# Conversion DMAs on GpSimd's queue, conversion steps in other iterations, a first pair started inside the first MLP, and another order inside a pair

## The chip, the cores and the metric

The kernel runs on one core of one Trainium2 chip. The metric is the device time of one execution in microseconds (us). TensorE (PE, its weight loads are PEld), VectorE (DVE), ScalarE (ACT), GpSimd (POOL) and SyncE (SP) each run their own list of instructions in order and wait for one another by semaphores; SP does nothing here but start DMAs (its queue is SPq).

## The reference

```python
kv = einsum('bhsd,bhse->bhde', k, v)            # q, k, v: 4 x 8 x 576 x 64, fp32
out = einsum('bhsd,bhde->bhse', q, kv)
attn = out / sqrt(mean(out * out, -1) + 1e-6) * g_norm
x = attn.transpose(0, 2, 1, 3).reshape(2304, 512)
gate = 1 / (1 + exp(-(x @ w_gate)))             # 512 -> 1536
y = (gate * (x @ w_val)) @ w_out                # 1536 -> 512, the first MLP
h = y @ w_in                                    # 512 -> 2048
g = max(h, 0) + log1p(exp(-abs(h)))
result = g @ w_out2                             # 2048 -> 512, the second MLP
```

All of it is fp32 in and out.

## The kernel before

**Products.** Each large product is made of three matmul passes over a high and a low part of both operands (`PASSES`, L22; `mm3`, L62). A tensor is split by an ACT copy to the high part (`split_hi`, L66) and a DVE subtraction for the low part (`split_lo`, L69).

**First MLP.** The 2304 tokens are cut into five tiles of 512, 512, 384, 384 and 512 (`TILES1`), each with 12 iterations, n = 0 to 59 in all. In iteration n PE multiplies x by a slice of the gate weights (12 matmuls into ps_g, `sigmoid` on ACT), by a slice of the value weights (12 into ps_v, `gated` L509 and `gated_lo` on DVE, a cast on ACT), and runs the output product of the iteration before (12 into yacc, `ffn1_out`). Other work is hung into this loop by `at_place(n, place, ...)`: "A", "B", "C" lie on PE behind the g, v and output products, "bg" and "b" behind the sigmoid and the gating, "end" ahead of the output product, "late" at the iteration's end. The attention of the next tile runs there, piece by piece: loads of q (16 DMAs a piece, L430) and of k and v (L252, L255), DVE transposes of q (L437), products po and kv_ps (L272), a root and a reciprocal (L481), the scaled rows of x.

**Conversion.** The weights of the second MLP arrive as 64-bit words and are made into fp32 on the chip, for j = 0 to 7, each an "i" part (w_in) and a "u" part (w_out2): `m_load` (4 or 2 DMAs, L582, L578), `m_a` (two ACT steps), `m_b` (two DVE steps of 128x1024, L596 and L599), for "i" also `m_sums` (four DVE adds that make the sums which the second MLP multiplies by), `m_h` (a cast on ACT), `m_l` (DVE), and `m_store` (L634, L628) into wi_dram and wu_dram. j takes iterations 12+5j to 16+5j, so the eight take 12 to 51. All these DMAs, and all others, are started by SP, in one line: a DMA that waits for its buffer or data holds those behind it. The raw words lie in home c0, m_f in c1 or c2, m_y in c2.

**Second MLP.** Three blocks of 768 tokens, 8 pairs each, 24 pairs. A pair forms 2 slices of h by seven products of 6 matmuls (128x384, two PSUM banks ps_b and ps_c), named by weight piece and sum of y: 11, 12, 22, S1 to S4 (`product`, L664). Copies on ACT (L1134, L1145, L1155, L1169) and additions on DVE (L1140, L1156, L1161) put them together. Softplus runs on ACT and DVE in steps of 128x768 (`s_abs` ... `s_lo`), and `out_group` (3 matmuls of 128x512, called a fill, 12 a pair) multiplies the pair before by w_out2 into oacc. The weights are read back by `feed_next` into `RING`, eight homes. The seven sums of y for a block lie in homes b0 to b6 (`COMBS`) as y_c; those of the next block are written over them when the last pair of a block is done with each (`combs`). `out_evac` copies oacc out and stores it.

**What sets the order.** The program text is the order of each engine. Names of lines that the prediction uses are in brackets above.

Of the kernel before, what the change touches and what calls it, by code (L numbers as in the profile page):

```python
# [30 lines left out]
def attention_moe_moe_kernel(ctx: ExitStack, tc: tile.TileContext, q, k, v, g_norm,  # L31
# [540 lines left out]
    m_x, m_f, m_y = {}, {}, {}  # L572

    def m_load(kind, j):
        m_x[kind, j] = x = block("c0", [P, 4, 256, 2], U32, "m_raw")
        if kind == "u":
            for f in range(2):
                nc.sync.dma_start(out=x[:, 2 * f:2 * f + 2].rearrange("p s c two -> p (s c two)"),  # L578
                                  in_=row_unit(w_out2, 2 * j + f))
        else:  # L580
            for f, kh, slot in ((1, 0, 0), (0, 0, 1), (0, 1, 2), (1, 1, 3)):
                nc.sync.dma_start(out=x[:, slot].rearrange("p (k m) two -> p k (m two)", k=2),  # L582
# [635 lines left out]
```

## Time and profile before

| | us |
|---|---|
| median of 3 runs (lowest, highest) | 949.48 (948.06, 953.69) |
| the profiled execution, its own time | 948.98 |
| its span in the profile | 947.2 |
| PE busy | 901.9 (95%) |
| DVE busy | 603.7 (64%) |
| ACT busy | 488.7 (52%) |
| POOL busy | 1.6 |

Three stretches of the span: tiles of 384 tokens, iterations 24 to 47, from 245 to 437.5 us; the last tile of the first MLP, from 437.5 to 534.8 us; the second MLP, from 534.8 us on. In the rows below, a line of the chain or of the timeline begins with the start and the length in us; "x12" is a count of instructions; a bracket holds the idle time of the engine before it and who ended it.

### The profile page before, as it was taken

The numbers are of one execution on the slowest core, as the hardware profiler recorded it, in microseconds if no ns is written. First come the engines' busy times: TensorE is split into PE (matmuls) and PEld (weight loads), VectorE is DVE, ScalarE is ACT, GpSimd is POOL, SyncE is SP. The second block draws the span as 40 slices with busy tenths as digits, with TensorE's granted clock in tenths as the row PEclk, the third lists the DMA queues.
The fourth block names the chain that finished last, engine by engine and source line by source line (L and its number), as shares of the span: only waits on it lengthen the run. The fifth ranks groups of instructions, "written<-read, shape, count | busy, mean of one in ns | idle before, by whom it ended". The sixth has DMA issues, their size and how long they took to land.

```text
span 947.2 us, 12188 instructions
## 1 busy us (share of the span) xinstructions
PE 901.9 (95%) x4701; PEld 785.0 (83%) x4701; DVE 603.7 (64%) x873; ACT 488.7 (52%) x771; POOL 1.6 (0%) x8
## 2 busy tenths in 40 slices
PE   8899999999988999999999989999799999799997
PEld 6687888788887989897888879888688988689896
DVE  4797846566875675687532256576675767657575
ACT  5887744445455454654322255556555555555553
POOL 0000000000000000000000000000000000000000
PEclk9999999999999999999999999999999999999999
DMA  9997367754678568755825536563286445265311
GB/s 303 271 338 234 133 216 230 215 199 172 194 225 268 206 173 264 225 203 205 283 72 196 185 125 240 182 247 153 90 295 236 190 166 219 79 258 207 148 45 67
DMA packets 108058, 188.50 MB, mean 199 GB/s; under 512 B 35936, under 2 KB 84320, under 8 KB 95712
## 3 DMA queue, kind: packets, MB, share of 16 engines
q1 hardware_dynamic: 106624, 186.94, 56.9%
q10 hardware_dynamic: 1376, 0.79, 0.3%
q8 instruction: 37, 0.61, 0.3%
q14 instruction: 21, 0.17, 0.1%
HBM read 148.90 MB, written 38.80 MB: 198 GB/s over the span
## 4 chain that ended last, share of the span: by engine, by line
PE 72%; DVE 10%; ACT 6%; DMA 6%; SPq 4%; issue 2%; DVEq 0%; ACTq 0%
PE oacc L62 18%; PE yacc L62 11%; PE ps_g L62 11%; PE ps_v L62 11%; PE ps_b L664 9%; PE ps_c L664 8%; DMA kv_raw<-in_v_dram 2%; SPq L117 1%; DMA m_raw<-in_moe_w_in_dram 1%; DVE y_c L69 1%; SPq L430 1%; DMA q_raw<-in_q_dram 1%; DVE ms L481 1%; DVE m_f L69 1%; DVE m_raw L596 1%
## 5 line engine op out<-in xcount | busy, mean ns | idle before, releaser
L62 PE MATMUL oacc<-w_up,g 128*128 128x512 f32 x864 | 221.0, 397 | 1.3 <-ACT g L66 0.7
L62 PEld LDWEIGHTS oacc<-w_up,g 128*128 128x128 f32 x864 | 162.6, 190 | 29.0 <-DVE g L69 1.2
L62 PE MATMUL ps_v<-x,w 128*128 128x512 f32 (+1 forms) x720 | 160.0, 370 | 3.1 <-DVE sg L509 1.8
L62 PE MATMUL yacc<-ghl,w 128*128 128x512 f32 (+1 forms) x720 | 162.6, 375 | 0.0
L62 PE MATMUL ps_g<-x,w 128*128 128x512 f32 (+1 forms) x720 | 160.3, 370 | 2.0 <-ACT x L396 0.9
L62 PEld LDWEIGHTS ps_g<-x,w 128*128 128x128 f32 x720 | 131.2, 189 | 20.4 <-DVE x L397 1.4
L62 PEld LDWEIGHTS ps_v<-x,w 128*128 128x128 f32 x720 | 129.5, 188 | 20.8 <-DVE sg L509 2.4
L62 PEld LDWEIGHTS yacc<-ghl,w 128*128 128x128 f32 x720 | 132.1, 191 | 16.9 <-DVE w L69 0.4
L664 PE MATMUL ps_b<-y_c,w_in 128*128 128x384 f32 x576 | 119.5, 341 | 13.9 <-ACT y_c L66 7.1
L664 PEld LDWEIGHTS ps_b<-y_c,w_in 128*128 128x128 f32 x576 | 103.1, 188 | 23.4 <-ACT y_c L66 8.8
L664 PE MATMUL ps_c<-y_c,w_in 128*128 128x384 f32 x432 | 89.8, 342 | 3.8 <-DVE c L1156 2.5
L503 ACT ACTIVATE sg<-ps_g 128x512 f32<-128x512 f32 (+1 forms) x60 | 33.3, 556 | 109.6 <-PE ps_g L62 105.1
L509 DVE TENSOR_TENSOR sg<-sg,ps_v 128x512 f32<-128x512 f32 (+1 forms) x60 | 37.9, 631 | 81.4 <-PE ps_v L62 77.7
L664 PEld LDWEIGHTS ps_c<-y_c,w_in 128*128 128x128 f32 x432 | 76.4, 190 | 12.8 <-DVE c L1156 7.9
L66 ACT CAST ghl<-sg 128x512 fp32r<-128x512 f32 (+1 forms) x60 | 34.6, 576 | 80.9 <-DVE sg L509 80.9
L671 ACT ACTIVATE e<-c 128x768 f32<-128x768 f32 x48 | 40.7, 847 | 64.0 <-DVE c L1161 63.3
L66 ACT CAST g<-c 128x768 fp32r<-128x768 f32 x48 | 40.2, 837 | 55.6 <-DVE c L696 55.6
L69 DVE TENSOR_TENSOR g<-c,g 128x768 fp32r<-128x768 f32 x48 | 45.8, 955 | 21.7 <-ACT g L66 21.7
L691 DVE SCALAR_TENSOR_TENSOR u<-u,ln 128x768 f32<-128x768 f32 x48 | 45.8, 954 | 15.5 <-ACT ln L683 15.4
L69 DVE TENSOR_TENSOR ghl<-sg,ghl 128x512 fp32r<-128x512 f32 (+1 forms) x60 | 38.2, 636 | 21.2 <-ACT ghl L66 20.9
L679 DVE TENSOR_SCALAR u<-e 128x768 f32<-128x768 f32 x48 | 26.7, 556 | 34.2 <-ACT e L675 34.2
L696 DVE TENSOR_TENSOR c<-c,u 128x768 f32<-128x768 f32 x48 | 46.0, 958 | 1.7
(124 smaller groups left out, 902.4 us busy)
## 6 DMA issues: line engine op xcount, KB each, us to landing
w_in<-wi_dram SPq DMA_DIRECT2D x42, 1024.0 KB, 6.8
w<-wo_dram SPq DMA_DIRECT2D x24, 1024.0 KB, 5.7
w_up<-wu_dram SPq DMA_DIRECT2D x24, 1024.0 KB, 4.8
m_raw<-in_moe_w_in_dram SPq DMA_DIRECT2D x32, 256.0 KB, 4.7
m_raw<-in_moe_w_out_dram SPq DMA_DIRECT2D x16, 512.0 KB, 4.2
wu_dram<-m_f SPq DMA_DIRECT2D x16, 512.0 KB, 3.2
w_raw<-in_moe_w_gate_dram SPq DMA_DIRECT2D x12, 512.0 KB, 8.8
w_raw<-in_moe_w_val_dram SPq DMA_DIRECT2D x12, 512.0 KB, 9.1
```

The source lines that it names most:

```text
L62: nc.tensor.matmul(out=ps, lhsT=lhs(a), rhs=rhs(b), start=start and n == 0, stop=stop and n == 2)
L66: nc.scalar.copy(out=hi, in_=src)
L69: nc.vector.tensor_tensor(out=lo, in0=src, in1=hi.bitcast(F32), op=ALU.subtract)
L117: nc.sync.dma_start(out=t, in_=unit(w, f))
L430: nc.sync.dma_start(out=t[32 * c:32 * c + 32, hp, :m].rearrange("p (g j) -> p g j", j=32), in_=q[b, 2 * hp + hh, s0:s0 + m, 32 * e:32 * e ...
L503: nc.scalar.activation(out=sg, in_=chain.pop(("g", t, i)), func=ACTF.Sigmoid)
L509: nc.vector.tensor_tensor(out=sg, in0=sg, in1=chain.pop(("v", t, i)), op=ALU.mult)
L664: nc.tensor.matmul(out=ps, lhsT=w[:, a, kk * P:(kk + 1) * P], rhs=y[:, b, kk], start=first and kk == 0 and n == 0, stop=kk == 1 and n == 2 ...
L671: nc.scalar.activation(out=e, in_=h_t[p][:, f], func=ACTF.Abs)
L679: nc.vector.tensor_scalar(out=u, in0=e_t[p, f], scalar1=1.0, scalar2=None, op0=ALU.add)
L691: nc.vector.scalar_tensor_tensor(out=u, in0=u, scalar=1.0, in1=ln_t.pop((p, f)), op0=ALU.subtract, op1=ALU.subtract)
L696: nc.vector.tensor_tensor(out=h, in0=h, in1=u_t.pop((p, f)), op=ALU.subtract)
```

## The change

**DMAs.** `m_load` and `m_store` are started by GpSimd (`nc.gpsimd`) and no longer by SP: 104 DMAs. For j from 5 on, the raw words and m_f of "u" have homes of their own (d0, d1), in room that the attention leaves.

**Iterations.** The rule 12+5j is replaced by the table `WHEN_J`. A row is (m_a and m_b of "i", m_sums, m_h and m_l of "i", m_a and m_b of "u", m_h and m_l of "u"); the last three rows have "u" one iteration behind "i".

**First pair.** Four products of pair 0 (11, 12, S2, S1) are in iteration 57, three (S3, S4, 22) in iteration 58, its softplus in 59.

**Sums of y.** Nine homes in turn instead of seven fixed ones, keyed by block, so that sums of the next block can be made in the last three pairs of a block (`gaps`). The ring has six homes instead of eight.

**Order in a pair.** 11, 12, S2, S1, S3, three fills, S4, 22, nine fills. A finished block is copied out in the second pair of the next. The last pair does its softplus in quarters of 128x384 (`quads`, `last_pair`), and the last groups are copied out one by one in the order 3, 4, 5, 0, 1, 2.

```diff
-    COMBS = ("11", "21", "T1", "T2", "22", "T3", "T4")
+    Y_HOME = ("b0", "b1", "b2", "b3", "b4", "b5", "b8", "b10", "b11")
...
     def m_load(kind, j):
-                nc.sync.dma_start(out=x[:, 2 * f:2 * f + 2].rearrange("p s c two -> p (s c two)"),
+                nc.gpsimd.dma_start(out=x[:, 2 * f:2 * f + 2].rearrange("p s c two -> p (s c two)"),
...
     def m_store(kind, j, a):
-                nc.sync.dma_start(out=wi_dram[g // 4][:, g % 4:g % 4 + m, a], in_=part[:, s:s + m])
+                nc.gpsimd.dma_start(out=wi_dram[g // 4][:, g % 4:g % 4 + m, a], in_=part[:, s:s + m])
...
-    RING = ("b7", "b8", "o0", "b9", "b10", "o1", "b11", "o2")
+    RING = ("b6", "b7", "o0", "b9", "o1", "o2")
...
-    for j in range(F2 // 2):
-        at_place(10 + 5 * j, "late", call(m_load, "i", j))
-        n = 12 + 5 * j
+    WHEN_J = ((9, 10, 11, 12, 13), (17, 18, 19, 20, 21), (25, 26, 28, 29, 30), (31, 32, 33, 34, 35),
+              (36, 37, 38, 39, 40), (48, 49, 50), (51, 52, 53), (54, 55, 56))
+    for j, (n, ns, nh, *nu) in enumerate(WHEN_J):
...
+    at_place(n0 + 9, "C", call(p_start, 0), call(p_11, 0), call(p_copy, 0), call(p_12, 0), call(p_add, 0, 0, 0, 0),
+             call(p_s2, 0), call(p_copy, 1), call(p_s1, 0))
+    at_place(n0 + 10, "A", call(p_s3, 0), call(p_copy, 2), call(p_add, 0, 1, 1, 2))
+    at_place(n0 + 10, "B", call(p_s4, 0), call(p_add, 0, 0, 1, 1))
+    at_place(n0 + 10, "C", call(p_22, 0), call(p_last, 0))
...
+            if j == NJ - 3:
+                return (call(y_sub, "T1", "12", "11", t_1), call(y_sub, "T2", "22", "T1", t_2)), \
+                       (call(y_diff, "T3", "22", "12", "12"),)
+            if j == NJ - 2:
+                return (call(y_split, "11"), call(y_split, "21")), (call(y_diff, "T4", "21", "T2", "21"),)
+            if j == NJ - 1:
+                return (call(y_split, "T2"), call(y_split, "T1"), call(y_hi, "T3"), call(y_hi, "22")), \
+                       (call(y_lo, "T3"), call(y_lo, "22"))
+        if j == 0 and p:
+            return (call(y_split, "T4"),), ()
...
+        p_start(p)
+        p_11(p)
+        s_lo(q, 0)
+        p_copy(0)
+        s_ln(q, 1)
+        for f in evac[:3]:
+            f()
+        p_12(p)
+        p_add(p, 0, 0, 0)
+        s_u2(q, 1)
+        p_s2(p)
+        s_sub(q, 1)
+        p_copy(1)
+        p_s1(p)
+        p_s3(p)
+        p_copy(2)
+        s_hi(q, 1)
+        p_add(p, 1, 1, 2)
+        s_lo(q, 1)
...
+        fill(3)
+        p_s4(p)
+        p_add(p, 0, 1, 1)
+        for f in gap_b:
+            f()
+        s_abs(p, 0)
+        s_exp(p, 0)
+        p_22(p)
+        p_last(p)
...
+        fill(99)
```

Place 1, SP around the loads of k, v and q for the last tile, with buffer numbers. First before, then after: L204 loads output weights of the first MLP, L255 k and v, L430 q, and L634 stores converted weights.

```order
L255 DMA kv_raw_2594<-in_k_dram 128x2x256
L255 DMA kv_raw_2594<-in_v_dram 128x2x256
L204 DMA w_2650<-wo_dram_90 128x2048
L634 DMA wi_dram_91<-m_y_2676 128x3x256
L634 DMA wi_dram_91<-m_y_2676 512x1x256
L255 DMA kv_raw_2711<-in_k_dram 128x2x256
L255 DMA kv_raw_2711<-in_v_dram 128x2x256
L634 DMA wi_dram_91<-m_f_2533 128x3x256
L634 DMA wi_dram_91<-m_f_2533 512x1x256
L255 DMA kv_raw_2745<-in_k_dram 128x2x256
L255 DMA kv_raw_2745<-in_v_dram 128x2x256
L430 DMA q_raw_2782<-in_q_dram 32x2x32 x16
```

```order
L255 DMA kv_raw_2563<-in_k_dram 128x2x256
L255 DMA kv_raw_2563<-in_v_dram 128x2x256
L204 DMA w_2624<-wo_dram_90 128x2048
L255 DMA kv_raw_2683<-in_k_dram 128x2x256
L255 DMA kv_raw_2683<-in_v_dram 128x2x256
L255 DMA kv_raw_2717<-in_k_dram 128x2x256
L255 DMA kv_raw_2717<-in_v_dram 128x2x256
L430 DMA q_raw_2759<-in_q_dram 32x2x32 x16
```

The four stores that stood between the loads of k and v are gone from SP; the loads keep their order.

They stand on POOL, whose list after the change reads here as follows (L593 and L589 load raw words, L645 and L639 store; j = 2 and the loads of j = 3 and of the "u" part).

```order
L593 DMA m_raw_2180<-in_moe2_w_in_dram 128x2x256 x4
L589 DMA m_raw_2362<-in_moe2_w_out_dram 128x1024 x2
L645 DMA wi_dram_91<-m_y_2566 128x2x256
L645 DMA wi_dram_91<-m_y_2566 512x1x256
L645 DMA wi_dram_91<-m_y_2566 128x256
L645 DMA wi_dram_91<-m_f_2344 128x2x256
L645 DMA wi_dram_91<-m_f_2344 512x1x256
L645 DMA wi_dram_91<-m_f_2344 128x256
L593 DMA m_raw_2722<-in_moe2_w_in_dram 128x2x256 x4
L639 DMA wu_dram_92<-m_f_2688 256x1x512 x2
```

POOL has no other work between them.

Place 2, PE at the end of the first MLP, first before, then after. The products ps_b and ps_c are those of pair 0 (before, from its tenth row on also of pair 1); the list of after begins at its first product.

```order
L62 MATMUL ps_v<-x,w 128x512 x12
L62 MATMUL yacc<-ghl,w 128x512 x12
L664 MATMUL ps_b<-y_c,w_in 128x384 x6
L664 MATMUL ps_c<-y_c,w_in 128x384 x6
L664 MATMUL ps_b<-y_c,w_in 128x384 x6
L62 MATMUL yacc<-ghl,w 128x512 x12
L664 MATMUL ps_c<-y_c,w_in 128x384 x6
L664 MATMUL ps_b<-y_c,w_in 128x384 x6
L664 MATMUL ps_c<-y_c,w_in 128x384 x6
L664 MATMUL ps_b<-y_c,w_in 128x384 x12
L664 MATMUL ps_c<-y_c,w_in 128x384 x6
L664 MATMUL ps_b<-y_c,w_in 128x384 x6
```

```order
L677 MATMUL ps_b<-y_c,w_in 128x384 x6
L677 MATMUL ps_c<-y_c,w_in 128x384 x6
L677 MATMUL ps_b<-y_c,w_in 128x384 x6
L677 MATMUL ps_c<-y_c,w_in 128x384 x6
L62 MATMUL ps_g<-x,w 128x512 x12
L677 MATMUL ps_b<-y_c,w_in 128x384 x6
L62 MATMUL ps_v<-x,w 128x512 x12
L677 MATMUL ps_c<-y_c,w_in 128x384 x6
L62 MATMUL yacc<-ghl,w 128x512 x12
L677 MATMUL ps_b<-y_c,w_in 128x384 x6
L62 MATMUL ps_g<-x,w 128x512 x12
L62 MATMUL ps_v<-x,w 128x512 x12
```

The seven products of pair 0 moved from behind the last ps_v to the place between the products of the last three iterations; after the last row shown come yacc x24 and the first product of pair 1.

Place 3, PE in pair 1, with buffer numbers, first before, then after. oacc is a fill, of pair 0; each product names the y_c that it reads.

```order
L664 MATMUL ps_b_4783<-y_c_4223,w_in_4536 128x384 x6
L664 MATMUL ps_c_4793<-y_c_4277,w_in_4584 128x384 x6
L664 MATMUL ps_b_4783<-y_c_4375,w_in_4584 128x384 x6
L62 MATMUL oacc_4816<-w_up_4538,g2_4784 128x512 x3
L664 MATMUL ps_c_4793<-y_c_4325,w_in_4584 128x384 x6
L62 MATMUL oacc_4817<-w_up_4538,g2_4784 128x512 x3
L664 MATMUL ps_b_4783<-y_c_4472,w_in_4630 128x384 x6
L62 MATMUL oacc_4818<-w_up_4538,g2_4784 128x512 x3
L62 MATMUL oacc_4819<-w_up_4538,g2_4784 128x512 x3
L664 MATMUL ps_c_4793<-y_c_4423,w_in_4630 128x384 x6
L62 MATMUL oacc_4820<-w_up_4538,g2_4784 128x512 x3
L664 MATMUL ps_b_4783<-y_c_4521,w_in_4584 128x384 x6
```

```order
L677 MATMUL ps_b_4788<-y_c_4167,w_in_4536 128x384 x6
L677 MATMUL ps_c_4799<-y_c_4225,w_in_4622 128x384 x6
L677 MATMUL ps_b_4788<-y_c_4402,w_in_4622 128x384 x6
L677 MATMUL ps_c_4799<-y_c_4346,w_in_4622 128x384 x6
L677 MATMUL ps_b_4788<-y_c_4521,w_in_4690 128x384 x6
L62 MATMUL oacc_4833<-w_up_4760,g2_4743 128x512 x3
L62 MATMUL oacc_4834<-w_up_4760,g2_4743 128x512 x3
L62 MATMUL oacc_4835<-w_up_4760,g2_4743 128x512 x3
L677 MATMUL ps_c_4799<-y_c_4461,w_in_4690 128x384 x6
L677 MATMUL ps_b_4788<-y_c_4577,w_in_4622 128x384 x6
L62 MATMUL oacc_4836<-w_up_4760,g2_4743 128x512 x3
L62 MATMUL oacc_4837<-w_up_4760,g2_4743 128x512 x3
```

The single fills between S2, S1 and S3 are gone, three fills stand together behind S3, and the rest behind 22.

## Rows read from the trace of the kernel before

**Rows 1.** Windows: stretch, its length, busy us (instructions) by engine, granted clock, DMA.

```profile
core 0: us, PE busy (x) PEld busy (x) DVE busy (x) ACT busy (x) POOL busy (x), PEclk, DMA share, GB/s
245.00:437.50 192.50, 177.15 (x1046) 168.46 (x1044) 133.05 (x235) 102.16 (x192) 0.00 (x0) 0.98 0.67 216
437.50:534.80 97.30, 97.30 (x432) 80.89 (x433) 39.24 (x52) 27.69 (x41) 0.00 (x0) 1.00 0.52 187
553.10:933.30 380.20, 367.91 (x1782) 324.53 (x1782) 251.03 (x327) 201.36 (x295) 0.00 (x0) 0.99 0.45 172
698.64:714.34 15.70, 15.70 (x80) 14.05 (x79) 10.01 (x13) 8.24 (x13) 0.00 (x0) 1.00 0.78 310
```

**Rows 2.** Chain of work: start us, us, engine, tile, line and count of matmuls.

```profile
332.38 2.08 PE ps_g L62 x12
...
535.99 1.04 PE ps_c L664 x6
...
642.34 4.80 PE oacc L62 x21
```

**Rows 3.** Waits of PE, 245 to 437.5 us: total, times, longest us.

```profile
PE po L62 <- ACT hl L66: 8.6, 10, 2.0
PE kv_ps L272 <- DMA kv_raw<-in_v_dram: 3.8, 2, 2.1
```

**Rows 4.** Chain of what released the stall at 274 us.

```profile
264.47 1.24 DVE m_f L599
...
265.76 0.37 SPq L582
...
267.71 2.07 SPq L430
```

**Rows 5.** Timeline, 274 to 432 us: start, us; in brackets idle time before, releaser.

```profile
274.29 0.81 PE L62 MATMUL po<-hl,kvb 128*128 128x160 f32 x3 [1.53 <-ACT hl L66]
...
295.33 0.98 SPq L634 DMA_DIRECT2D wi_dram<-m_y  x2
...
306.61 0.95 PE L272 MATMUL kv_ps<-kv_raw 128*64 128x64 f32 x20 [1.77 <-DMA kv_raw<-in_v_dram]
...
307.49 3.86 PE L62 MATMUL yacc<-ghl,w 128*128 128x384 f32 x12
...
424.72 1.22 DVE L596 SCALAR_TENSOR_TENSOR m_raw<-m_raw 128x1024 uint32<-128x1024 uint32 x1
...
432.08 2.35 PE L62 MATMUL ps_v<-x,w 128*128 128x384 f32 x12 [1.85 <-DVE sg L509]
```

**Rows 6.** Chain of work between the two MLPs.

```profile
534.92 1.06 PE ps_b L664 x6
...
543.49 0.57 DVE c L1156
...
553.09 1.82 PE ps_b L664 x6
```

**Rows 7.** Chain of work: fills of 21 matmuls around the two block boundaries.

```profile
698.64 4.80 PE oacc L62 x21
...
777.27 4.80 PE oacc L62 x21
...
834.34 4.80 PE oacc L62 x21
```

**Rows 8.** Waits of PE's weight loads, 553.1 to 933.3 us: total, times, longest.

```profile
PEld ps_c L664 <- DVE c L1156: 6.4, 21, 1.1
```

**Rows 9.** Timeline of PE in the last 20 us.

```profile
928.38 4.96 PE L62 MATMUL oacc<-w_up,g 128*128 128x512 f32 x21
...
935.36 8.00 PE L62 MATMUL oacc<-w_up,g 128*128 128x512 f32 x34 [0.61 <-DVE g L69]
```

**Rows 10.** Source line L634, its DMA issues on SP: ns minimum/median/maximum, first and last start.

```profile
L634 SPq DMA_DIRECT2D wi_dram<-m_f x20: 320/560/1575, 166.1 to 455.2; - x20
```

**Rows 11.** The page's costliest groups: busy us, mean ns, idle before.

```profile
L69 DVE TENSOR_TENSOR g<-c,g 128x768 fp32r<-128x768 f32 x48 | 45.8, 955 | 21.7 <-ACT g L66 21.7
```

More of the change, by code (lines that the diff above doesn't have):

```diff
@@ new lines, in attention_moe_moe_kernel, with p_open @@
+    at_place(n0 + 5, "end", call(y_split, "T1"), call(y_diff, "T2", "22", "T1", "T1"))
+    at_place(n0 + 6, "end", call(y_split, "T2"), call(y_diff, "T4", "21", "T2", "21"))
+    at_place(n0 + 7, "end", call(y_split, "22"))
+    at_place(n0 + 8, "end", call(y_split, "T3"))
+    at_place(n0 + 9, "b", call(y_split, "T4"))
+    for n in (7, 8, 9, 10, 11):
+        at_place(n0 + n, "late", feed_next)
+    p_c, p_t = {}, {}
+    def p_open():
+        more.close()
+        p2.append(ctx.enter_context(tc.tile_pool(name="p2a", bufs=1, side="right")))
+        p_t["t2"] = p2[0].tile([P, 2, HT], F32, tag="t2", name="t_2")
+        for n in range(3):
+            p_c[n] = block(f"c{n}", [P, 4 * 512], F32, "c")
@@ new lines, in h_of, with p_part, p_bank, p_copy @@
+    def h_of(p):
+        return p_c[p % 2][:, :2 * TM2].rearrange("p (f s) -> p f s", f=2)
+    def p_part(n):
+        return p_c[2][:, HT * n:HT * (n + 1)]
+    def p_bank(p, name):
+        pool, tag = (mm, "mm") if p else (atp, "at")
+        p_t[name] = pool.tile([P, 512], F32, tag=tag, name="ps_" + name)[:, :HT]
+    def p_copy(n):
+        nc.scalar.copy(out=p_part(n), in_=p_t["b"])
+    def p_add(p, f, th, n):
+        nc.vector.tensor_tensor(out=h_t[p][:, f, HT * th:HT * (th + 1)], in0=p_t["c"], in1=p_part(n), op=ALU.add)
@@ new lines, in p_last, with p_start, p_11, p_12 @@
+    def p_last(p):
+        nc.scalar.copy(out=h_t[p][:, 1, :HT], in_=p_t["b"])
+    def p_start(p):
+        h_t[p] = h_of(p)
+        p_bank(p, "b")
+    def p_11(p):
+        product(p, p_t["b"], "11", "11", True)
+    def p_12(p):
+        p_bank(p, "c")
+        product(p, p_t["c"], "12", "21", True)
+    def p_s2(p):
+        product(p, p_t["b"], "S2", "T2", False)
+    def p_s1(p):
+        product(p, p_t["c"], "S1", "T1", True)
+    def p_s3(p):
+        product(p, p_t["b"], "S3", "T3", False)
@@ L1066, in attention_moe_moe_kernel @@
             at.close()
+            more_pool.append(more.enter_context(tc.tile_pool(name="more", bufs=1, side="right")))
     assert not work
-    xs.close()
-    p2 = ctx.enter_context(tc.tile_pool(name="p2", bufs=1))
-    nc.scalar.preload_act_table_set("natural_log_exp_and_others")
-    ca, cb, cc = (block(f"c{n}", [P, 4 * 512], F32, "c") for n in range(3))
-    h_buf = [x[:, :2 * TM2].rearrange("p (f s) -> p f s", f=2) for x in (ca, cb)]
-    p1, u2, u3 = (cc[:, HT * n:HT * (n + 1)] for n in range(3))
@@ new lines, in attention_moe_moe_kernel @@
+    ffn1_out(*its[-1][1:])
+    feed_to(0)
+    for _ in range(2):
+        og = g1pool.tile([P, 2, 512], F32, tag="g", name="ob")
+        obs += [og[:, 0], og[:, 1]]
+    for p in range(1, NPAIR + 1):
+        q = p - 1
+        t, j = divmod(p, NJ)
+        evac = [call(out_evac, q - 1, s) for s in range(NS2)] if j == 1 and t else []
+        q_fill = [call(out_group, q, f, s) for f in range(2) for s in range(NS2)]
+        if p == NPAIR:
+            for n in range(NS2):
+                out_group(q, 0, n)
+            for n in (3, 4, 5, 0, 1, 2):
+                out_group(q, 1, n)
+                out_evac(q, n)
@@ L1181, in attention_moe_moe_kernel @@
         fill(99)
[L1182 to L1187 removed]
+        feed_to(p)
 _INS = ['q', 'k', 'v', 'g_norm', 'moe_w_gate', 'moe_w_val', 'moe_w_out', 'moe2_w_in', 'moe2_w_out']
```

264 lines of the change are left out of this document (151 added, 113 removed).

## The prediction

> **What bounds the kernel now.** I read the page first: PE is busy for 901.9 of 947.2 us, DVE for 603.7, ACT for 488.7. PE has the most work, and no PE work is added or removed, so whatever the change gains must come out of PE's gaps and of the stretches where PE runs at a lower clock. I then cut the span into stages with the windows view. The last tile of the first MLP has no gap (97.30 of 97.30 us at a granted clock of 1.00). The two tiles of 384 tokens have 15.35 us of gaps in 192.50, at a clock of 0.98. The second MLP from pair 1 on is busy for 367.91 of 380.20 us [rows 1]. The chain of work gives the dense pace there: 12 matmuls of 384 columns take 2.08 us, a product of 6 takes 1.04, and 21 matmuls of 512 take 4.80, so one of 512 takes 0.229 [rows 2]. A pair is 7 products and 36 fill matmuls: 7 × 1.04 + 36 × 0.229 = 15.5 us. A measured pair takes 15.70, with DVE busy for 10.01 and ACT for 8.24 of it [rows 1].
>
> The losses lie in five places. I cost each one against the profiled execution's own time, 948.98 us (1.78 outside its span of 947.2, and 0.5 below the median of 949.48; I call this the same).
>
> **A, the order within a pair: 4 us.** S4 waits for the addition L1156 that frees ps_c: 6.4 us over 21 pairs, 0.3 each [rows 8]. In the new order three fills stand between S3 and S4, 3 × 3 × 0.229 = 2.06 us, in which ACT's copy and that addition (0.57, [rows 6]) fit. A pair then runs at its floor of 15.5 instead of 15.7, and about 20 of the 23 pairs behind pair 0 are plain ones: 20 × 0.2 = 4. Between 0 and 6.4.
>
> **B, the two block boundaries: 17 us.** From the fill at 642.34 to that at 698.64 are 56.30 us for what would be three pairs of 15.70, 47.1, and a second entry makes one more step: 9.2 us lost [rows 2, 7]. At the other boundary, 777.27 to 834.34, it is 57.07 − 47.1 = 9.97 [rows 7]. Sum 19.2. In that time the splits of y's sums stand in the last pair and the first, since each has to wait for its home. With nine homes they are spread over three pairs, four of them in the fullest one. A split costs DVE 0.955 us (the nearest row, [rows 11], the same 768 columns), so DVE needs 10.01 + 4 × 0.955 = 13.8 of 15.5 us there, which fits. I leave 1 us at each boundary: 17. If all four splits stay unhidden at each, 19.2 − 2 × 3.8 = 11.6, so 12 to 19.
>
> **C, the way into the second MLP: 7 us.** Pair 0's first product is at 534.92, pair 1's at 553.09: 18.17 us [rows 6]. PE's work in between is 7 × 1.04 and the last 12 yacc matmuls at 0.229, 10.0 together, so 8.2 are lost while pair 1 waits for pair 0's softplus. In the new program the seven products stand between full products of the last iterations and the softplus lies beside iteration 59, in which DVE was busy for 39.24 of 97.30 us [rows 1]. Pair 1's first five products, 5.2 us, need nothing of it. I take 7, for one late step. If four DVE steps of 0.955 are still not covered it is 4.4, so 4 to 8.2.
>
> **D, the end: 1.6 us.** 21 matmuls begin at 928.38 and the last 34 at 935.36 [rows 9]. At 4.80 us for the 21 and 0.46 for two between them, 6.98 − 5.26 = 1.7 us are lost waiting for the last pair's softplus. Quarters of 384 columns should be ready by then: 1.6, between 0 and 1.7. The last copy and its store stay.
>
> **E, the stalls in the tiles of 384 tokens: 12 us.** The stretch holds 15.35 us of gaps and, at a mean clock of 0.98, 0.02 × 192.5 = 3.9 us of slow running: 19.2 [rows 1]. Most gaps are in po, 8.6 us, and in kv_ps, 3.8 [rows 3]. Two places show SP's one line as the cause. At 264.47 DVE runs its last step on c0's words; only then can SP start m_raw (265.76), and q's 16 loads behind it begin at 267.71; po then waits 1.53 us at 274.29 [rows 4, 5]. At 295.33 a store of m_y, which waits for the cast, stands ahead of the loads of k and v; kv_ps waits twice, 3.8 in all, and the yacc behind it takes 3.86 us instead of 2.08 [rows 2, 3, 5]. That is 1.53 + 3.8 + 1.78 = 7.1, and with the DMAs on GpSimd all of it should go. The other 12.1 are put down to DVE's steps: m_b at 424.72 stands ahead of the gating for which ps_v waits 1.85 us at 432.08 [rows 5]. Before, 10 m_b steps lie in iterations 24 to 47 (12+5j and 15+5j); in the table 6 do (25, 29, 31, 34, 36, 39). I take 4 of 10 of 12.1, 4.8: together 11.9, say 12. The three conversions in iterations 48 to 56 I cost at nothing: they stand beside a stretch without a gap where DVE has 58 us free. Each is two m_b (2.45 us), four sums, m_l twice, some 10 us, 30 in all. Without that cover they would stall as in the tiles before, about 1.2 us for each of 6 m_b. Bounds of E: the kv places alone, 5.3, and the whole 19.2.
>
> **What the moved DMAs cost on GpSimd.** No row shows a DMA started by POOL. The nearest rows are the same stores on SP: 0.320, 0.560 and 1.575 us to start one [rows 10]. The densest place is j = 5 to 7: 40 DMAs in nine iterations of 97.30/12 = 8.1 us, 73 us, so POOL becomes the bound only from 1.82 us a DMA on. I take the median, 0.56, and cost it at nothing; POOL has nothing else to do. From below the bound is nothing too.
>
> **Sum.** 4 + 17 + 7 + 1.6 + 12 = 41.6, and 948.98 − 41.6 = 907.4 us. With all bounds at their best, 6.4 + 19.2 + 8.2 + 1.7 + 19.2 = 54.7: 894. At their worst, 0 + 12 + 4 + 0 + 5.3 = 21.3: 927.7.
>
> **The rivals.**
>
> *The queue move buys nothing.* The loads are late because the transfers are slow, not because SP's line stands still. For it: the DMA engines are busy for 0.67 of that stretch [rows 1], and the same bytes still have to move. Against it: q's first load is started 1.95 us behind m_raw's first, right when that one is let go [rows 4]. The 7.1 us then stay: 914.5. The Trainium skill, page “DMA: Bandwidth & Descriptors”, section “Issuing engines are not separate DMA queues”, says that DMAs from several engines end on the same 16 DMA engines and that spreading the issue only saves the sequencer's time. By that rule this rival is right wherever the line waits for nothing; the rows of this case show a line that waits for a buffer, which the rule does not speak of.
>
> *The new order stalls.* S1 now follows S2 at once, so the addition that frees ps_c (0.57 us, [rows 6]) must run within S2's 1.04 us. For it: DVE has a split of 0.955 ahead of it [rows 11]. If the split begins late, S1 waits about 0.5 us in each of 20 pairs, 10 us lost and the 4 of A not gained: 921.4. Against it: that split only needs a cast issued a pair earlier, and 12 and 11 give it 2.08 us.
>
> *GpSimd's queue is too slow* (the other side). If a DMA costs POOL 3 us, the 14 of a late j take 42 us where its three iterations have 24.3; the w_in and w_up of pairs 5 to 7 come late, and 3 × 17.7 = 53 us are added: 960.5, slower. It decides from 1.82 us on, and breaks even at about 1.82 + 41.6/40 = 2.9. Against it: the slowest of 20 starts in [rows 10] is 1.575. The Trainium skill, same page, section “Latency and other measured facts”, gives about 1 us to the first byte for GpSimd's path and about 0.6 for SP's; no row here shows it, and by it each moved DMA would only land 0.4 us later, which the iteration between load and use covers.
>
> **How the numbers follow.** Chances: the forecast 0.60, queue move without gain 0.17, order stalls 0.12, GpSimd too slow 0.08, anything else 0.03. The forecast is **907.4 us**. The range from 893 to 928 takes in the bounds of the sum and the first two rivals, and leaves out about the last two cases and a little on both sides. A measurement of this kernel can tell about 1% from no change: faster means below 940, slower above 958.5. Faster: 0.60 + 0.17 + 0.12, less a little for mishaps that add up, 0.87. Same 0.05, slower 0.08.
>
> **What would show it.** A: no wait of ps_c for its addition, pairs 15.5 apart. B: fills 15.7 apart across both boundaries, with 1 us over. C: no PE gap between the last yacc and pair 1. D: the last fills follow on each other. E: kv_ps without a wait and po below 5 us in the stretch of 384 tokens; its length about 180 us. The prediction is wrong if ps_g, ps_v or yacc wait in iterations 48 to 59, if POOL's DMAs land later than their use, or if w_in or w_up has to be waited for with a ring of six.

## The result and the profile after

The changed kernel takes 900.65 us (median of 4 runs, 899.67 to 902.06), the kernel before 948.77 beside it (947.89 to 953.69): a ratio of 0.9484, 95% interval 0.9448 to 0.952. The forecast was 907.4 us with a range from 893 to 928. The profiled execution, the fastest of the four, took 899.67 us with a span of 897.9, 49.3 less than the span before.

PE is now busy for 882.9 of 897.9 us (98%). First the windows view of the changed kernel, cut at the same places of the program as before: iterations 24 to 47, iterations 48 to 59 with pair 0, and the pairs from 1 on. The columns are those of [rows 1].

```profile
core 0: us, PE busy (x) PEld busy (x) DVE busy (x) ACT busy (x) POOL busy (x), PEclk, DMA share, GB/s
244.40:417.40 173.00, 169.11 (x1046) 165.23 (x1045) 117.21 (x217) 89.37 (x181) 26.23 (x38) 1.00 0.60 194
417.40:526.00 108.60, 108.19 (x488) 90.51 (x487) 61.80 (x79) 48.39 (x63) 24.46 (x36) 1.00 0.66 237
526.00:879.50 353.50, 353.09 (x1768) 319.10 (x1767) 251.34 (x330) 199.21 (x298) 0.00 (x0) 1.00 0.54 203
```

Iterations 24 to 47 had 15.35 us of gaps at a clock of 0.98 [rows 1]; now they have 3.9 (173.00 − 169.11) at 1.00. From pair 1 on, PE has 0.4 us of gaps in 353.50, where 12.3 in 380.20 stood before. The gaps of the first of these stretches are two waits, in PE's waits of the changed kernel (total, times, longest, in us):

```profile
PE kv_ps L272 <- DMA kv_raw<-in_v_dram: 2.6, 1, 2.6
PE po L62 <- ACT hl L66: 1.0, 1, 1.0
```

po waited 8.6 us before and kv_ps 3.8 [rows 3]. The chain of work of the changed kernel shows the pairs (start us, us; 27 fill matmuls end each pair):

```profile
536.49 6.16 PE oacc L62 x27
...
552.07 6.16 PE oacc L62 x27
...
630.02 6.16 PE oacc L62 x27
...
645.72 6.16 PE oacc L62 x27
...
864.09 6.16 PE oacc L62 x27
...
879.67 14.34 PE oacc L62 x63
```

A plain pair takes 552.07 − 536.49 = 15.58 us, where it took 15.70. The block boundary stands between 630.02 and 645.72: 15.70, so 0.1 us over a plain pair, where the two pieces of [rows 2, 7] lost 9.2 and 9.97. The last 63 fill matmuls of the kernel run in one piece.

The two traces can be cut at the same instructions:

| from, to | before, us | after, us | less | predicted |
|---|---|---|---|---|
| start, first ps_g of iteration 24 | 245.04 | 244.39 | 0.65 | 0 |
| ..., first ps_g of iteration 48 (E) | 191.73 | 172.94 | 18.8 | 12 |
| ..., pair 1's first product (C) | 116.32 | 108.62 | 7.7 | 7 |
| ..., end of pair 1's fills (C) | 15.41 | 16.70 | −1.3 | |
| ..., end of pair 22's fills (A, B) | 349.14 | 327.60 | 21.5 | 4 + 17 |
| ..., end of the span (D) | 29.56 | 27.65 | 1.9 | 1.6 |
| sum | 947.2 | 897.9 | 49.3 | 41.6 |

Of the 21.5 us, 21 pairs at 0.12 each are A, 2.5; the other 19.0 are B. Nearly all of the gain that was not forecast lies in one row, E.

### The profile page after: what moved, and what is told of

The parts are those of the page before. It is cut to its first block, busy times and chain, and to the rows that moved or that the text cites. A ratio compares the mean times of both kernels' runs of the same rounds, so it can differ in the third digit from the quotient of the medians.

```text
span 897.9 us, 12246 instructions
## 1 busy us (share of the span) xinstructions
PE 882.9 (98%) x4701; PEld 779.4 (87%) x4701; DVE 604.4 (67%) x884; ACT 486.9 (54%) x778; POOL 73.0 (8%) x112
## 3 DMA queue, kind: packets, MB, share of 16 engines
q0 software_dynamic: 11392, 39.85, 12.5%
## 4 chain that ended last, share of the span: by engine, by line
PE 82%; DMA 7%; DVE 4%; ACT 2%; SPq 2%; issue 1%; POOL 0%; DVEq 0%; ACTq 0%
PE oacc L62 22%; PE yacc L62 13%; PE ps_g L62 13%; PE ps_v L62 12%; PE ps_b L677 11%; PE ps_c L677 8%; DMA kv_raw<-in_v_dram 3%; DMA wo_dram<-w 1%; SPq L117 1%; PE po L62 1%; PE kv_ps L272 1%; DMA q_raw<-in_q_dram 1%; DVE w_raw L145 1%; DMA w_raw<-in_moe_w_out_dram 1%; DMA kv_raw<-in_k_dram 1%
## 5 line engine op out<-in xcount | busy, mean ns | idle before, releaser
L62 PE MATMUL oacc<-w_up,g 128*128 128x512 f32 x864 | 205.2, 391 | 0.0
L62 PE MATMUL yacc<-ghl,w 128*128 128x512 f32 (+1 forms) x720 | 160.3, 371 | 0.4 <-DVE ghl L69 0.2
L62 PEld LDWEIGHTS yacc<-ghl,w 128*128 128x128 f32 x720 | 129.7, 188 | 17.9 <-ACT ghl L66 0.6
L677 PE MATMUL ps_b<-y_c,w_in 128*128 128x384 f32 x576 | 116.4, 336 | 0.1
L677 PE MATMUL ps_c<-y_c,w_in 128*128 128x384 f32 x432 | 87.5, 337 | 0.3 <-DVE c L1075 0.3
L1075 DVE TENSOR_TENSOR c<-ps_c,c 128x384 f32<-128x384 f32 x72 | 40.0, 556 | 61.7 <-ACT c L1072 32.5
L1072 ACT COPY c<-ps_b 128x384 f32<-128x384 f32 x72 | 34.6, 480 | 82.0 <-PE ps_b L677 80.3
L66 ACT CAST g<-c 128x768 fp32r<-128x768 f32 (+1 forms) x50 | 40.6, 812 | 32.1 <-DVE c L714 28.2
L709 DVE SCALAR_TENSOR_TENSOR u<-u,ln 128x768 f32<-128x768 f32 x46 | 43.8, 953 | 12.2 <-ACT ln L701 12.2
```

What stands on the lines that cost most here:

```text
L62: nc.tensor.matmul(out=ps, lhsT=lhs(a), rhs=rhs(b), start=start and n == 0, stop=stop and n == 2)
L66: nc.scalar.copy(out=hi, in_=src)
L677: nc.tensor.matmul(out=ps, lhsT=w[:, a, kk * P:(kk + 1) * P], rhs=y[:, b, kk], start=first and kk == 0 and n == 0, stop=kk == 1 and n == 2 ...
L709: nc.vector.scalar_tensor_tensor(out=u, in0=u, scalar=1.0, in1=ln_t.pop((p, f)), op0=ALU.subtract, op1=ALU.subtract)
L1072: nc.scalar.copy(out=p_part(n), in_=p_t["b"])
L1075: nc.vector.tensor_tensor(out=h_t[p][:, f, HT * th:HT * (th + 1)], in0=p_t["c"], in1=p_part(n), op=ALU.add)
```

## The experiments

Times are compared by their ratio to the kernel before that ran beside them; a difference from the changed kernel is that of the ratios times 949.5, and the two intervals leave some 4 us on it. "The stretch" is the time from the first ps_g of iteration 24 to that of iteration 48.

### Where the gain in the stretch comes from: four runs

The two edits of the conversion, its queue and its iterations, were undone one at a time and both, in the changed kernel; and the queue alone was changed in the kernel before.

```diff
 # e1 (and e3): in m_load and m_store
-                nc.gpsimd.dma_start(...)
+                nc.sync.dma_start(...)
 # e2 (and e3)
-    WHEN_J = ((9, 10, 11, 12, 13), ..., (54, 55, 56))
+    WHEN_J = [tuple(range(12 + 5 * j, 17 + 5 * j)) for j in range(8)]
-    N_LATE = 5
+    N_LATE = 8
 # e4: in m_load and m_store of the kernel before
-                nc.sync.dma_start(...)
+                nc.gpsimd.dma_start(...)
```

New iterations, DMAs on SP:

> The changed kernel with only the queue undone: m_load and m_store start their DMAs on SP again, the conversion stays in the iterations of the new table. In the changed kernel iterations 24 to 47 take 173.0 us (244.4 to 417.4) where the kernel before took 192.5, 19.5 less. Theory L (SP's one line held the loads of q, k and v back, and that is most of it): the loads are late again, po and kv_ps wait 8 us or more in that stretch, and the time rises by 8 to 13 us, to 909 to 914. Theory T (the other iterations are most of it, since fewer DVE steps lie there): it rises by less than 4, to 901 to 904. Theory E (either of the two is enough by itself): 901 to 904 as well; the next runs tell T and E apart.

Old iterations, DMAs on GpSimd:

> The changed kernel with only the table undone: the conversion lies in iterations 12+5j to 16+5j again, its DMAs stay on GpSimd's queue. Theory L: 1 to 5 us over the changed kernel, 902 to 906. Theory T: 12 us or more over it, from 912 on, with ps_v and po waiting behind m_b on DVE. Theory E: 901 to 904.

Both undone:

> The changed kernel with both undone: conversion in iterations 12+5j to 16+5j and its DMAs on SP. By every theory the 19.5 us of the stretch come back, 918 to 921 us; below 915 a part of the gain in this stretch came from something else (the y loads, the feeds, the room in the homes).

The kernel before with GpSimd's queue:

> The kernel before with only the queue changed: m_load and m_store start their DMAs on GpSimd. Theory L: 8 to 14 us under the kernel before, 935 to 941, with kv_ps without a wait. Theory T: 3 to 7 us under it, 942 to 946. Theory E: 15 us or more under it, below 934. If a DMA cost GpSimd some 3 us it would be slower than before.

| kernel | median us | ratio (95%) | over the changed kernel | the stretch, us | PE busy in it | PE's waits there: po, kv_ps |
|---|---|---|---|---|---|---|
| changed | 900.65 | 0.9484 (0.9448 to 0.952) | | 172.94 | 169.05 | 1.0, 2.6 |
| e1: new iterations, SP | 910.75 | 0.9583 (0.9559 to 0.9606) | 9.4 | 180.44 | 173.25 | 3.8, 3.0 |
| e2: old iterations, GpSimd | 916.59 | 0.9649 (0.9627 to 0.9672) | 15.7 | 186.45 | 173.47 | 7.2, 0.4 |
| e3: old iterations, SP | 920.02 | 0.9687 (0.9667 to 0.9707) | 19.3 | 192.20 | 176.72 | 8.9, 3.6 |
| e4: kernel before, GpSimd | 948.11 | 0.9981 (0.9965 to 0.9998) | | 186.95 | 173.47 | 7.9, 0.3 |
| before | 948.77 | 1 | | 191.73 | 176.61 | 8.6, 3.8 |

No theory had it whole. Undoing both gives back 19.3 us, and the stretch is 192.20 again, so the two edits are all of E. (The homes d0 and d1, `N_LATE`, went with the iterations here and were not undone alone.) Theory E (either is enough) is out: each alone leaves about half of the loss or more. Theory L had the time of e1 (9.4 in its 8 to 13) but not its waits (6.8 us where it said 8 or more), and was wrong on e2 and e4; theory T was right on e2 and wrong on e1 and e4 (1.8 us gained where it said 3 to 7). By the times, the queue is worth 19.3 − 15.7 = 3.6 us with the old iterations (give or take 3) and 9.4 with the new ones (give or take 4); the stretches of the single traces give 5.8 and 7.5. That the two edits work together is likely, and only just clear of the noise.

The waits show the parts. Those of po go with the iterations (8.9 us in e3, 3.8 in e1). Those of kv_ps go with the queue at the old iterations (3.6 in e3, 0.4 in e2), and hardly at the new ones (3.0 in e1, 2.6 in the changed kernel). A stretch read from one trace is good to some 3 us only: e5 to e9 below leave it as it is and show 171.8 to 178.0 us, with waits like those of the changed kernel; what differs most is PE's busy time, 169.1 to 173.3 us, at a granted clock of 1.00 to 0.97.

What the queue does directly is in the PE timeline of e1 (start, us; in brackets the idle time before and its releaser):

```profile
275.84 0.81 PE L62 MATMUL po<-hl,kvb 128*128 128x160 f32 x3 [0.64 <-ACT hl L66]
...
301.70 1.53 PE L272 MATMUL kv_ps<-kv_raw 128*64 128x64 f32 x20 [3.05 <-DMA kv_raw<-in_v_dram]
```

kv_ps waits 3.05 us for v and po 0.64 for q's cast, in the same two places as before [rows 5]. SP's line can account for little of the first, as kv_ps waits 2.6 us there in the changed kernel too. Of the 7.5 us by which e1's stretch is longer, 3.3 are gaps, 2.8 of them po's, and 4.2 are PE's longer busy time, at a clock of 0.98. In this profiled execution, whose span is 911.0 us, another 4.7 us lie ahead of iteration 24 (its first ps_g is at 249.12, in the changed kernel at 244.39). The queue doesn't make them all: 2.3 are there at 85 us (a ps_g at 87.81 that stands at 85.54 in the changed kernel), and e1 starts its first conversion DMA at 93.1. The rest comes between 147 and 159 us, where po waits twice, 1.6 us in all.

Why the queue gives so little with the old iterations is in the timeline of e4 at the end of iteration 47:

```profile
429.09 1.14 ACT L126 ACTIVATE m_raw<-m_raw 128x1024 f32<-128x1024 f32 x1 [3.82 <-DMA m_raw<-in_moe_w_in_dram]
...
431.12 2.16 ACT L66 CAST x<-of 128x512 fp32r<-128x512 f32 x4
...
431.77 0.49 PE L62 MATMUL ps_g<-x,w 128*128 128x512 f32 x1 [2.92 <-ACT x L66]
```

ACT's first conversion step (L126) waits 3.82 us for raw words that GpSimd's queue brought; the cast of the next tile's x stands behind it on ACT, and PE waits 2.92 us for that cast. The first of the four loads was started at 420.07, 9.0 us ahead of the step. Before, these were 6.8 us (427.26 and 434.09), and PE hardly waited (timeline of the kernel before):

```profile
436.77 0.50 PE L62 MATMUL ps_g<-x,w 128*128 128x512 f32 x1 [0.25 <-ACT x L66]
```

About 1 us of the difference is that POOL took 2.89 us to start the four and SP 1.92; the rest is open. Right behind the wait the granted clock falls, in the windows view of e4 (429 to 440 us, columns as in [rows 1]):

```profile
429.00:440.00 11.00, 8.00 (x28) 6.28 (x29) 6.14 (x9) 5.30 (x8) 1.11 (x2) 0.84 0.15 60
```

0.84 in 11 us, 1.8 us lost on top. Of the 4.8 us by which the stretch is shorter in e4, these 1.8 go first; another 2.1 are lost at its two block boundaries (57.76 and 57.67 us between the fills that stood 56.30 and 57.07 apart before, [rows 2, 7]), where no DMA of GpSimd runs; why is open. So the stall at this place grows while that of kv_ps goes (3.8 to 0.3 us) and po's stay (8.6 to 7.9). In the table of the changed kernel no conversion step stands in iterations 41 to 47, and nothing of it can be late there.

### How much of it is the two conversions in iterations 41 to 51

```diff
-              (36, 37, 38, 39, 40), (48, 49, 50), (51, 52, 53), (54, 55, 56))
+              (36, 37, 38, 39, 40), (52, 53, 54, 55, 56), (42, 43, 44, 45, 46), (47, 48, 49, 50, 51))
-    N_LATE = 5
+    N_LATE = 8
```

> The changed kernel with two of the eight conversions put back to where j = 6 and 7 were before, iterations 42 to 46 and 47 to 51 (four m_b steps more before iteration 48), and one in 52 to 56; the rows at 9 to 40 stay as changed. All DMAs on GpSimd. With the whole old rule the time rose by 16 us. Theory M (what counts is beside which attention steps an m_b lies; those of the last tile's rms rows lie in 41 to 47): 6 to 9 us over the changed kernel, 906.5 to 909.5, with gaps at iterations 42 to 48. Theory N (every m_b costs about the same, 12.1 us over 10 of them): 4 to 5 us over it, 904.5 to 905.5.

911.53 us, ratio 0.9574 (0.9552 to 0.9597), 8.5 over the changed kernel; the stretch takes 180.05 us, 7.1 more. That is theory M. At an even 1.2 us for each m_b it would have been 3.6, since three more lie before iteration 48 by the table (42, 45 and 47), and not four as the expectation has it. The margins, 4 us on the 8.5 and 3 on a stretch, make theory M the likelier one and don't rule theory N out. The timeline of e10 shows the last two stalls of PE, and ACT's step ahead of the second:

```profile
418.07 3.91 PE L62 MATMUL ps_v<-x,w 128*128 128x384 f32 x12 [1.82 <-DVE sg L509]
...
422.91 1.12 ACT L126 ACTIVATE m_raw<-m_raw 128x1024 f32<-128x1024 f32 x1 [3.96 <-DMA m_raw<-in_moe_w_in_dram]
...
425.57 0.50 PE L62 MATMUL ps_g<-x,w 128*128 128x512 f32 x1 [1.49 <-ACT x L66]
```

ps_v waits 1.82 us for a gating that stands behind m_b and two reciprocals on DVE (as at 432.08 in [rows 5]), and then runs 3.91 us instead of 2.08. The second is the place of e4: the cast of x stands behind a conversion step that waited 3.96 us for its raw words. The windows view of its last 26 us:

```profile
400.00:426.00 26.00, 22.69 (x118) 21.55 (x116) 18.31 (x21) 12.07 (x17) 8.36 (x12) 0.93 0.65 232
```

3.3 us of gaps, and a granted clock of 0.93 for 26 us, 1.8 more. At the place itself 5.1 us are seen. Of the 13.5 us that the new iterations are worth in the stretch (186.45 − 172.94), by single traces 7.1 are the two conversions and the other 6.4 the shift of the rows between 24 and 40, where six m_b steps stand instead of seven.

### Could the stretch be shorter still

```diff
-    WHEN_J = (..., (25, 26, 28, 29, 30), ...)
+    WHEN_J = (..., (22, 23, 24, 25, 26), ...)
```

> The changed kernel with the third conversion in iterations 22 to 26 instead of 25 to 30, so that its m_b, its stores and the loads of the fourth lie off the place at 295 us where kv_ps waits 2.58 us for v. If the transfers and DVE steps of that conversion make the wait, 1.5 to 2.5 us under the changed kernel, 898 to 899; if the wait is that of the two homes of the loads, no difference within 0.7.

900.05 us, ratio 0.946 (0.9444 to 0.9476): within the interval of the changed kernel. The stretch takes 172.04 us, 0.9 less; kv_ps no longer waits in it, and po waits a little in four places. The wait of kv_ps was that conversion's: the changed kernel and e5 to e9 all show it, 1.6 to 2.9 us. In the time it can't be told: 2.3 us less by the ratios, 0.6 by the medians, where the expectation had 1.5 to 2.5 or no difference.

### The order of the fills

```diff
         p_copy(1)
+        fill(1)
         p_s1(p)
+        fill(1)
         p_s3(p)
...
-        fill(3)
+        fill(2)
         p_s4(p)
...
         s_exp(p, 0)
+        fill(1)
         p_22(p)
```

> The changed kernel with the fills back between the products of a plain pair (one behind S2, one behind S1, two ahead of S4, one ahead of 22, the rest behind 22), all else as changed. If the order of the fills is what took a pair from 15.70 to 15.58 us, the 20 plain pairs lose 0.1 to 0.3 us each, 2 to 6 in all: 902.5 to 906.5. If something else did (the softplus steps that were moved with it, the evacuation), it stays within 1.5 of 900.65.

914.21 us, ratio 0.9627 (0.9601 to 0.9653), 13.6 over the changed kernel: far more than expected. The chain of e5 gives a plain pair:

```profile
538.93 4.80 PE oacc L62 x21
...
554.63 4.80 PE oacc L62 x21
```

15.70 us again, so the place of the fills is what A's 0.12 us a pair come from, 2.5 us in all. The other 11 lie around the boundaries: from the fill at 586.03 to that at 685.50, and from 716.96 to 815.63, six pairs each take 99.47 and 98.67 us where six plain ones take 94.2, 9.7 us together. PE's waits of e5 in the second MLP name 7.0 of them:

```profile
PE oacc L62 <- DVE ob L742: 4.4, 2, 2.2
PE ps_b L677 <- ACT c L1072: 2.1, 6, 0.4
PE oacc L62 <- DMA w_up<-wu_dram: 0.5, 1, 0.5
```

A fill right behind S2 is the first to write oacc of a new block, and it now comes before the finished block has been copied out: 4.4 us. Another 2.1 are six short waits for a copy on ACT, and 2.7 of the 9.7 stay open. The order and the moved copies belong together; the prediction had treated them apart.

### The block boundaries

```diff
 # e6: gaps(p) as combs(p) was: 11, 21, T2, T1 split in the last pair, T3, 22 and the difference T4 in the next
 # e7: the same, and
-    Y_HOME = ("b0", "b1", "b2", "b3", "b4", "b5", "b8", "b10", "b11")
+    Y_HOME = ("b0", "b1", "b2", "b3", "b4", "b5", "b8")
```

> The changed kernel with nine homes, but with the splits of y's sums where they stood before: four in the last pair of a block, three and the difference T4 in the first pair of the next. Theory P (the place of the splits caused the 19.2 us at the boundaries): 12 to 19 us over the changed kernel, 913 to 920, with waits for y_c. Theory H (seven homes caused it, the splits had to wait for products to be done): less than 5 over it, below 906.

> As the run before it, and with seven homes in turn instead of nine. Theory P: the same time as with nine homes within 3 us. Theory H: 12 to 19 us over the changed kernel, and 8 or more over the run with nine homes.

e6 takes 921.04 us, ratio 0.9695 (0.9679 to 0.9711), 20 over the changed kernel; e7 922.19, 0.9703 (0.9684 to 0.9721). That is just above theory P's 12 to 19 and far from theory H's 5; e7 is within P's 3 us of e6. Theory P holds. The chain around the first boundary, e6 and then e7:

```profile
614.88 6.16 PE oacc L62 x27
...
671.45 6.16 PE oacc L62 x27
```

```profile
617.46 6.16 PE oacc L62 x27
...
674.08 6.16 PE oacc L62 x27
```

Three pairs of 15.58 are 46.7; 671.45 − 614.88 = 56.57, so 9.8 us are lost, and 9.9 in e7. PE's waits of e6:

```profile
PE ps_b L677 <- ACT y_c L66: 6.2, 2, 3.1
PE ps_b L677 <- DVE y_c L69: 2.8, 4, 1.1
```

The sums of y are late, as before. Of the 9.8 us at the first boundary of e6, 5.3 are gaps; in the other 4.5 PE runs longer (51.29 us busy in 56.57), at a clock of 0.94. Two homes more change nothing while the splits stand where they stood. By the program they are what lets the splits be put earlier: with seven, 11's new sum would be written over the one that the next pair still reads. That is not shown: new places with seven homes were not tried.

### The first pair

```diff
-    at_place(n0 + 9, "C", call(p_start, 0), call(p_11, 0), ...)
 ...
-    at_place(n0 + 11, "end", call(s_max, 0, 0), ...)
 # and behind the loop of the first MLP: the seven products of pair 0, the last yacc behind S2, its softplus
```

> The changed kernel with the first pair behind the first MLP, as before: its seven products with the last yacc between them, then its softplus, then pair 1. The prediction took 7 us for this part (4 to 8.2): 907.7 us, with 8 us between pair 0's last product and the pace of pair 1, and a wait for ACT's cast or copy ahead of pair 1. If pair 0's softplus inside the last iteration only moved the loss, it stays below 903.

907.28 us, ratio 0.9546 (0.9531 to 0.956), 5.9 over the changed kernel. PE's waits of e8 in the second MLP:

```profile
PE ps_b L677 <- ACT c L1072: 4.5, 1, 4.5
PE ps_c L677 <- DVE c L1075: 1.2, 1, 1.2
```

These two, 5.7 us, are the wait for pair 0's softplus and the addition ahead of S4, as at 553.09 and 544 us before [rows 6].

### The last pair

```diff
-        if p == NPAIR - 1:
-            last_pair(p)
-            continue
 # and ahead of the last fills: s_lo(q, 0), s_ln, s_u2, s_sub, s_hi and s_lo of (q, 1)
```

> The changed kernel with the last pair done like any other: its softplus in steps of 128x768 and its second half behind the products, as before; the order of the last copies stays. The prediction took 1.6 us for the end (0 to 1.7): 902.2. Within 0.5 of 900.65, and the quarters buy nothing; from 903 on, and the end was worth more than the gap between the fills at 928.38 and 935.36 showed.

903.98 us, ratio 0.9496 (0.9479 to 0.9514), 1.1 over the changed kernel by the ratios; the intervals overlap, so the time doesn't settle the expectation. The end of its trace shows it without that noise (timeline of PE in e9):

```profile
886.06 7.10 PE L62 MATMUL oacc<-w_up,g 128*128 128x512 f32 x29
893.76 8.01 PE L62 MATMUL oacc<-w_up,g 128*128 128x512 f32 x34 [0.60 <-DVE g L69]
```

From the end of pair 22's fills to the end of the span are 28.9 us, 1.3 more than in the changed kernel (27.65). In e9 the stretch alone was 5 us longer than in the changed kernel, with the same two waits (kv_ps 2.8, po 1.5); 4.3 of it are PE's busy time, 173.34 us at a clock of 0.97. So this execution's time says little on the end.

### A slow queue on GpSimd

```diff
+    def slow_pool():
+        for _ in range(3):
+            nc.gpsimd.dma_start(out=slow_dram[n_slow[0]:n_slow[0] + 1], in_=g_norm.rearrange("(a d) -> a d", a=1))
+            n_slow[0] += 1
 ...                                   # ahead of each of the 104 DMAs
+                slow_pool()
```

> The changed kernel with GpSimd's queue slowed: three more small DMAs (256 bytes, from g_norm to a scratch row in memory that nobody reads) ahead of each of the 104. A DMA took GpSimd 0.55 to 0.86 us in the changed kernel, so each of the 104 now takes some 2.6 to 2.9 us of its time. By the working of the rival on a slow queue it binds from 1.82 us on: 14 x 2.75 = 38.5 us for a late j that has 24.3, 14 x 3 = 43 us more, 935 to 950. If the ring, the distance between conversion and use, or the later pairs take it up, it is under 910: pair 5's weights are only needed some 80 us after the last store.

944.8 us, ratio 0.9934 (0.9909 to 0.996), 42.7 over the changed kernel. The time is in the range that the rival's working gave, but the place is another. The added DMAs in the groups of POOL in e11:

```profile
L590 POOL DMA_DIRECT2D slow_dram<-in_g_norm_dram x312 | 157.8, 544 | 19.9 <-DMA slow_dram<-in_g_norm_dram 12.2 <-issue 7.5
```

157.8 + 77.7 us for the 104 real ones are 2.26 us for each of 104. The stretch takes 17.3 us more and the part from iteration 48 to pair 1's first product 24.3 more, nearly all in the first MLP; no product waits for w_in or w_up later. The timeline of e11 late in the last tile:

```profile
519.54 1.22 DVE L620 SCALAR_TENSOR_TENSOR m_f<-m_raw 128x1024 uint32<-128x1024 uint32 x1 [14.66 <-DMA wi_dram<-m_f]
...
522.42 0.68 DVE L509 TENSOR_TENSOR sg<-sg,ps_v 128x512 f32<-128x512 f32 x1
...
523.15 1.22 PE L62 MATMUL ps_v<-x,w 128*128 128x512 f32 x2 [9.73 <-DVE sg L509]
```

DVE's m_b (L620) waits 14.66 us for a store to let go of its home, with y's splits and the gating behind it, and PE waits 9.73 for the gating. A late DMA is felt at once, by what stands behind the waiting step on DVE or ACT. But starting is not all that made these DMAs late: between 460 and 540 us POOL is busy for 56.5 of 80, and among its waits are earlier transfers of its own queue, 12.2 us in the added DMAs alone.

## Why the prediction was right, and where its size was off

**A, order within a pair, 4 us: 2.5.** The wait of ps_c is gone, and e5 shows that the place of the fills does it. The pair is 15.58 us and not 15.5: its 36 fills take 2.08 + 6.16 = 8.24 us, the rest is the seven products. Costing the order by itself was wrong: the same edit holds up the moved copies of a block and the boundaries, 11 us more in e5.

**B, boundaries, 17: 19.0.** Right, and by the mechanism given. I left 1 us at each boundary; the trace leaves 0.1. DVE had room for four splits in a pair.

**C, way into the second MLP, 7: 6.4.** 7.7 up to pair 1, less 1.3 in pair 1, and 5.9 by e8. The one late step that was allowed for is seen in the timeline of the changed kernel, in pair 1:

```profile
525.95 1.23 PE L677 MATMUL ps_b<-y_c,w_in 128*128 128x384 f32 x6
...
528.35 1.32 PE L677 MATMUL ps_b<-y_c,w_in 128*128 128x384 f32 x6
529.95 1.31 PE L677 MATMUL ps_c<-y_c,w_in 128*128 128x384 f32 x6 [0.28 <-DVE c L1075]
```

S2 starts 2.40 us behind 11 where two products take 2.08, and S1 waits 0.28 for the addition: DVE and ACT still have pair 0's softplus and the copies of the last yacc there.

**D, the end, 1.6: 1.9** by the cut traces, 1.3 by e9's.

**E, the tiles of 384 tokens, 12: 18.8, the step that was mis-sized.** Its queue part, 7.1, has the size of the 7.5 us that e1's stretch is longer, but not its parts, so that agreement is partly luck. All 3.8 us of kv_ps were to go, and 2.6 stay; what the queue took away beside the new iterations is 2.8 us of po, 0.4 of kv_ps and 4.2 of slow running. With the old iterations, for which the 7.1 was worked out, it took 5.8 (e2 and e3) and 4.8 us (e4) out of the stretch, and 3.6 and 1.8 out of the time. (The lower bound of E, 5.3, is called the kv places alone; these are 3.8 + 1.78 = 5.6.) Its other part failed: I put 12.1 us evenly on ten m_b steps and took 4 of 10. The runs point to what stands behind an m_b as its cost. Beside reciprocals and q's transposes of the last attention pieces (iterations 41 to 47) two conversions cost 7.1 us, and at the rows between 24 and 40 a shift by some iterations took away another 6.4, though six of seven m_b steps are still there. Which step made each of those 6.4 us was not told apart. The upper bound of 19.2 was right: nearly the whole of the stretch's losses went. Slow running went with the gaps in this trace, where the clock is 1.00 in every row; e9, with the same edits in this stretch, had 0.97 in it.

**The moved DMAs at nothing.** Right in the changed kernel: (73.0 − 1.6)/104 = 0.69 us of POOL each, where 0.56 was taken, and POOL idles between them. A source line of it (nanoseconds minimum/median/maximum):

```profile
L645 POOL DMA_DIRECT2D wi_dram<-m_f x20: 557/756/809, 143.1 to 492.8; - x20
```

Compare 320/560/1575 on SP [rows 10].

**The conversions in iterations 48 to 56 at nothing.** Right: PE has 0.4 us of gaps in that stretch.

**The rivals.** That the queue buys nothing was wrong by 9.4 us in this kernel. The rule of the Trainium skill, page “DMA: Bandwidth & Descriptors”, section “Issuing engines are not separate DMA queues”, comes close to what the queue gave in the kernel before (1.8 us, e4), but for another reason than that rule's: kv_ps's wait for its loads went (3.8 to 0.3 us), and a late conversion step on ACT, with the block boundaries, took most of the time back. That S1 would stall each pair did not come: plain pairs have no wait. GpSimd's queue too slow did not come, with 0.69 us a DMA. At 2.26 us, in e11, the queue is too slow. The 1.82 that was worked out lies between the two and is neither confirmed nor refuted, as starting was not all that held e11's queue up. And the loss is in another place: in the steps of the first MLP and not in the weights of late pairs.

## What to carry to other kernels

A queue that starts DMAs in order should not hold transfers that wait for a buffer ahead of loads that are needed soon; but move such DMAs together with the steps that wait for them: here either edit alone gave about half of what both gave, or much less. Price a moved step by what stands behind it on its engine at the new place and at the old one, not by an average over all such steps. Where a sum must be rebuilt at a boundary, an extra buffer is worth only as much as it lets the rebuilding start earlier.

## What the runs showed of the hardware that was not expected

The same bytes moved in far fewer packets. First the page of the kernel before, then that of the changed kernel (queues with packets, MB and share of 16 engines; issues with KB each and median us to landing):

```profile
q1 hardware_dynamic: 106624, 186.94, 56.9%
...
m_raw<-in_moe_w_in_dram SPq DMA_DIRECT2D x32, 256.0 KB, 4.7
...
wu_dram<-m_f SPq DMA_DIRECT2D x16, 512.0 KB, 3.2
```

```profile
q1 hardware_dynamic: 76288, 147.08, 47.0%
q0 software_dynamic: 11392, 39.85, 12.5%
...
m_raw<-in_moe_w_in_dram POOLq DMA_DIRECT2D x32, 256.0 KB, 5.6
...
wu_dram<-m_f POOLq DMA_DIRECT2D x16, 512.0 KB, 5.9
```

SP's queue has 30336 packets fewer, and GpSimd's 11392 carry the same 39.85 MB. e2 and e4 have the packets of the changed kernel and e1 and e3 those of the kernel before, so it is the queue that sets them. The engines were busy with them for about as long: 0.125 × 897.9 = 112 us of 16 engines, where SP's queue gave up 0.569 × 947.2 − 0.470 × 897.9 = 117. A store of wu_dram lands 5.9 us after its issue instead of 3.2, and the raw words of w_in 5.6 instead of 4.7. Part of that is due to the other iterations, as the pages of e4 and then e1 show, which each have only one of the two edits of the conversion:

```profile
m_raw<-in_moe_w_in_dram POOLq DMA_DIRECT2D x32, 256.0 KB, 4.5
...
wu_dram<-m_f POOLq DMA_DIRECT2D x16, 512.0 KB, 4.5
```

```profile
m_raw<-in_moe_w_in_dram SPq DMA_DIRECT2D x32, 256.0 KB, 5.5
...
wu_dram<-m_f SPq DMA_DIRECT2D x16, 512.0 KB, 4.5
```

By the queue alone the store lands 1.3 us later at the old iterations (3.2 to 4.5) and 1.4 at the new ones (4.5 to 5.9); the raw words land at the same time within 0.2 us (4.7 and 4.5, 5.5 and 5.6). The Trainium skill, page “DMA: Bandwidth & Descriptors”, section “Latency and other measured facts”, gives about 0.6 us to the first byte for the one path and about 1 us for the other; the difference, some 0.4 us, is an estimate from these two. The whole transfers here show more than that for the store and nothing of it for the load, beside other traffic.
